# An mLSTM and MLP kernel: items of three pairs in the steady part, a third bank for h, and two banks that scores, sums with v, state update and transposes share

## The chip, the cores and the metric

The kernel runs on one core of one Trainium2 chip. The metric is device time in microseconds (us) of one execution of the whole program; the time before is the median of three runs.

A core has a matrix engine (TensorE, PE in the profile, with its weight loads as PEld), three engines for elementwise work (VectorE or DVE, ScalarE or ACT, GpSimd or POOL) and a queue engine for transfers (SP). They run side by side and wait for each other by semaphores. Products land in PSUM, which has eight banks of 128 partitions x 512 fp32 numbers; everything else lies in SBUF.

## The reference, cut to what matters

```python
# q, k, v: (4, 8, 768, 40); i_gate, f_gate: (4, 8, 768)
for t in range(S):
    m_new = np.maximum(f_gate[:, :, t] + m, i_gate[:, :, t])
    f_stab = np.exp(f_gate[:, :, t] + m - m_new)
    i_stab = np.exp(i_gate[:, :, t] - m_new)
    m = m_new
    C = f_stab[:, :, None, None] * C + i_stab[:, :, None, None] * np.einsum('bhd,bhe->bhde', vt, kt)
    n = f_stab[:, :, None] * n + i_stab[:, :, None] * kt
    h_tilde = np.einsum('bhde,bhe->bhd', C, qt)
    nq = np.einsum('bhd,bhd->bh', n, qt)[:, :, None]
    y[:, :, t] = o * h_tilde / np.maximum(np.abs(nq), 1.0)     # o: sigmoid of o_gate
# x: (3072, 320), tokens by heads and features; w_in: (320, 2048); w_out: (2048, 320)
h = x @ w_in
g = h - np.tanh(h)
out = g @ w_out
```

All of it is fp32. An attention part (the recurrence, done in chunks) makes x, and an MLP with the activation h - tanh(h) makes the output.

## The kernel before, in words

**Tiling.** The 3072 tokens are 24 units of 128 tokens (one batch entry, one chunk of 128 steps). Two units are a group of 256 tokens, so there are 12 groups. The 2048 hidden features are 8 pairs of two blocks of 128. The MLP's work is therefore 12 x 8 pairs (group g, pair p).

**Up.** For one pair, h needs for each of its two blocks i three products into 128 x 256 numbers: two with 128 rows of x (j = 0, 1) and one with the last 64 rows (320 = 128 + 128 + 64). The 64 rows of block 0 lie in the lower half of the array's rows and those of block 1 in the upper half, so two such half products can run at the same time (row tiles). `up` (L748) makes the lists: `full` with the products of 128 rows, and `rest` with the halves.

**Shrink.** `shrink_steps` (L768) makes g from h by a polynomial: per bank of h one square on ACT (which also adds up into a column of `sums`, for a later check of h's size), a second square on ACT, and on DVE a step `cube`, which is the last reader of the bank, and a step `product`. `Clock.later` (L141) puts the DVE steps into the order some time after the squares.

**Down.** For groups 4 to 10 (`SEVEN`), g @ w_out for 2 x 2 blocks is done with seven products in place of eight: `sums_of_weights` (L665) prepares sums of w_out's blocks on DVE (wT, once per pair), `sums_of_g` (L676) sums of g's (s1 to s4; s4 has one buffer), `down_seven` (L687) runs the products of 128 x 160 into three banks, and `put_together` (L722) adds them up. The other groups use `down` (L803) with four products of 128 x 320 per pair.

**Attention of a unit.** `scores` (L552): eight products of 40 rows, also in two row tiles, into two banks, then two masks on DVE. `inter` and `intra` (L577, L586): ph, sums with the state and with v. `gate` (L591): five DVE steps that make y. `update` and `keep_state` (L603, L611): pc, the state, for units that have a later chunk (the last four have none). `turn` and `keep_x` (L620, L628): three transposes px and an ACT copy into xT.

**Order.** All three compute engines run in the order in which the Python code issues (`Pinned`, `T`). The first part (groups 0 to 3, 12 units) is laid out by a planner (`Plan`). From `START` on the steady part is a loop over items (L1125): 64 pairs, in items of two. One item is: its full up products; then the halves together with the scores of a new unit, if one begins (`halves`, L568: products of all parts first, then the shrink steps and masks); then the down products of the item before (LAG = 1). `merge` (L833) strews the remaining attention work of `cell_slot` (L632) between these: 13 slots are spread evenly over the items.

**Banks.** `ph0` and `ph1` take h of an item: bank i holds block i of its pairs. `po0`, `po1` and `b1` take the down sums, `a0` and `a1` the scores, and `b0` in turn ph, pc and px (`small`, L258; `banks[:] = ["b0"]`, L1123).

Of the kernel before, what the change touches and what calls it, by code (L numbers as in the profile page):

```python
# [49 lines left out]
FP = mybir.dt.float32  # L50
# [4 lines left out]
AF = mybir.ActivationFunctionType  # L55
OP = mybir.AluOpType
PSUM = bass.MemoryType.PSUM
NO_SYNC = mybir.DependencyInfo(mybir.DependencyClass.NoSync, mybir.DependencyReason.DATA)

L = 128  # L60
# [18 lines left out]
def kernel(  # L79
# [173 lines left out]
    ps_a = ctx.enter_context(tc.tile_pool(name="ps_a", bufs=1, space=PSUM))  # L253
    ps_b = ctx.enter_context(tc.tile_pool(name="ps_b", bufs=1, space=PSUM))

    banks = ["b0", "b1"]

    def small(shape, name):  # L258
        banks.append(banks.pop(0))
        return ps_b.tile(shape, FP, name=name, tag=banks[-1])  # L260

# [58 lines left out]


    probe = const.tile([128, 1], FP, name="probe")
    V.memset(probe, 0.0)
    A.activation(out=probe, in_=probe, func=AF.Exp)
    ident = const.tile([128, 128], FP, name="ident")
# [328 lines left out]
        return steps + 2 * pause  # L654


    gT, po = {}, {}

# [14 lines left out]

    def sums_of_g(some):  # L676
        a = [[gT[some][i][:, :, tt * L:(tt + 1) * L] for i in range(2)] for tt in range(GT)]
        s1, s2, s3 = (conv.tile([128, 2, L], FP, name=name, tag=tag, bufs=2)[:, 0:len(some)]
                      for name, tag in (("s1", "w_e"), ("s2", "w_m"), ("s3", "w_r")))
        s4 = mlp.tile([128, 2, L], FP, name="s4", tag="s4", bufs=1)[:, 0:len(some)]  # L680
        gS[some] = s1, s2, s3, s4
        V.tensor_tensor(out=s3, in0=a[0][0], in1=a[1][0], op=OP.subtract)
        V.tensor_tensor(out=s1, in0=a[1][0], in1=a[1][1], op=OP.add)
        V.tensor_tensor(out=s2, in0=s1, in1=a[0][0], op=OP.subtract)
        V.tensor_tensor(out=s4, in0=a[0][1], in1=s2, op=OP.subtract)
# [62 lines left out]
    def up(some, shrink):  # L748

        n = len(some)  # L750
        ph = [ps_h.tile([128, 2, TG], FP, name="ph_up", tag=f"ph{i}") for i in range(2)]

        def product(i, x, j):
            g, p = some[x]
            f = 2 * p + i
            at = ((0, 2, 1), (0, 1, 2))[i][j]
            if j < NK:
                lhs, rhs = w_in[:, p, (2 * j + i) * 128:(2 * j + i + 1) * 128], xT[g % NX][:, at, :]
            else:
                rows = slice(i * HALF, (i + 1) * HALF)  # L760
                lhs, rhs = w_in[rows, p, 2 * NK * 128:], xT[g % NX][rows, at, :]
            T.matmul(ph[i][:, x, :], lhs, rhs, start=(x == 0 and j == 0), stop=(j == NK), skip_group_check=True)

        full = [(0.43, lambda i=i, x=x, j=j: product(i, x, j)) for i in range(2) for x in range(n) for j in range(NK)]
        rest = [lambda i=i, x=x: product(i, x, NK) for x in range(n) for i in range(2)]
        return full, (rest, [lambda: shrink(some, ph)])

    def shrink_steps(x, some, ph):  # L768

        n = len(some)  # L770
        z, q = ([mlp.tile([128, 2, TG], FP, name=name, tag=name)[:, 0:n] for i in range(2)] for name in ("z", "q"))
        gt = gT[some] = [mlp.tile([128, 2, TG], FP, name="gt", tag="gt", bufs=4)[:, 0:n] for i in range(2)]

        def square(i):
            A.activation(out=z[i], in_=ph[i][:, 0:n], func=AF.Square, accum_out=sums[:, 2 * x + i:2 * x + i + 1])

        def again(i):
            A.activation(out=q[i], in_=z[i], func=AF.Square, bias=tiny)

        def cube(i):  # L780
            V.scalar_tensor_tensor(out=gt[i], in0=ph[i][:, 0:n], scalar=TINY_POLY[0], in1=z[i], op0=OP.mult, op1=OP.mult)

        def product(i):
            V.scalar_tensor_tensor(out=gt[i], in0=q[i], scalar=TINY_POLY[2], in1=gt[i], op0=OP.add, op1=OP.mult)

        return square, again, cube, product

    def shrink(x):
        def steps(some, ph):
            n = len(some)  # L790
            square, again, cube, product = shrink_steps(x, some, ph)
            for step in (square, again):
                for i in range(2):
                    step(i)
            for i in range(2):
                Clock.later(some, 0.9 + 0.35 * n * i, lambda i=i: cube(i))
                Clock.later(some, 1.0 + 0.75 * n + 0.35 * n * i, lambda i=i: product(i))
            if some[0][0] in SEVEN:
                Clock.later(some, 1.01 + 1.1 * n, lambda: sums_of_g(some))

        return steps

# [54 lines left out]
    items = []  # L857
    while sum(map(len, items)) < len(pairs):
        x = sum(map(len, items))
        items.append(pairs[x:x + (1 if x in ALONE else 2)])  # L860

    assert 2 * len(items) == NS

    def item(x):

# [253 lines left out]
        x0, x1 = (START + (last - START) * j / len(slots) for j in (i, i + 1))  # L1119
        begins[int(x0)].append((slot, x0, x1))  # L1120
    for p in range(NP):
        spread_over([(0.0, lambda p=p: [step() for _, step in sums_of_weights(p)])], START + p / 2, START + 0.5 + p / 2)
    banks[:] = ["b0"]  # L1123
    load_unit(PLANNED)
    for x in range(START, len(items) + LAG):  # L1125
        dense, new = [], []
        for slot, x0, x1 in begins[x]:
            spread_over(cell_slot(*slot), x0, x1)
            if slot[0] is not None:
                new.append(slot[0])  # L1130
# [19 lines left out]

    def rows_of_f():

        xr, n, f = (mlp.tile([L, 2, NR], FP, name=name, tag=tag) for name, tag in (("xr", "z"), ("n", "z"), ("f", "q")))
# [16 lines left out]
        grow = mlp.tile([NR, 2, L], FP, name="grow", tag="gt", bufs=4)  # L1170
        zero = mlp.tile([NR, L], FP, name="zero", tag="gt", bufs=4)
# [65 lines left out]
    lead, root, _, rest = POLY  # L1237

    def shrink_any(ph):
        z = mlp.tile([128, 2, TG], FP, name="z", tag="z")  # L1240
        q = mlp.tile([128, 2, TG], FP, name="q", tag="q")
        t, big = (att.tile([128, 2, TG], FP, name=name, tag="P", bufs=4) for name in ("t", "big"))
        gt = mlp.tile([128, 2, TG], FP, name="gt", tag="gt", bufs=4)
# [11 lines left out]
    with tc.If(nc.values_load(again, min_val=0, max_val=128,  # L1255
                              skip_runtime_bounds_check_because="it counts partitions") > 0):
        T.last = V.last = A.last = None
        banks[:] = ["b0", "b1"]
        un.clear()
        G.tensor_copy(out=diag, in_=ident.unsqueeze(1).to_broadcast([128, H, L]))  # L1260
        V.tensor_copy(out=ei[:, 0], in_=ei[:, 1])
# [88 lines left out]
```

## Time and profile before

| | |
|---|---|
| median of 3 runs | 555.47 us (554.23 to 556.2) |
| profiled execution | 555.52 us, of which 553.7 us lie between its first and its last instruction (the span) |
| TensorE clock granted | 0.997 |
| DMA over the span | 37.97 MB, mean 69 GB/s |
| steady part | 220.8 us to about 547 us |

The busy shares in the page are averages over the whole span. PE records are pipelined: a record's end is modelled and lies after the start of the next, so that lengths in the timeline are read from start to start. An fp32 product leaves two records. `ph_up` is h, `pS` the seven sums, `po` the other down sums, `ps` the scores.

One line of the page on DVE and one on ACT, for the size of the shrink steps:

```profile
L106 DVE SCALAR_TENSOR_TENSOR gt<-ph_up,z 128x512 f32<-128x512 f32 (+1 forms) x100 | 63.3, 662 | 93.1 <-ACT z L106 92.9
...
L106 ACT ACTIVATE q<-z,tiny 128x512 f32<-128x512 f32 (+1 forms) x100 | 64.7, 700 | 0.0
```

After the name of the group stand its count, busy us, mean ns of one, and the engine's idle us before it with what ended most of that.

### The profile page before, as it was taken

How to read it: one execution, taken by the hardware profiler on the slowest of the kernel's cores; microseconds unless marked ns; L12 is line 12 of the kernel's file. 1: busy time of each engine (PE TensorE's matmuls, PEld its weight loads, DVE VectorE, ACT ScalarE, POOL GpSimd, SP SyncE). 2: the span in 40 equal slices, each digit the busy share in tenths (PEclk: the TensorE clock that was granted, in tenths of full speed). 3: DMA queues.
4: the chain of work that ended last, by engine and by line, in shares of the span. 5: the costliest groups of instructions: out<-in, count | busy, mean ns of one | idle time of the engine just before them, and what ended most of it. 6: DMA issues, size and time to landing. Idle time of an engine off the chain costs nothing.

```text
span 553.7 us, 8979 instructions
## 1 busy us (share of the span) xinstructions
PE 539.0 (97%) x3378; PEld 455.6 (82%) x3380; DVE 345.7 (62%) x754; ACT 179.8 (32%) x447; POOL 34.2 (6%) x67
## 2 busy tenths in 40 slices
PE   6999999999999999999999999999999999999995
PEld 4768878787877776798899999999989989988873
DVE  4699888989754335767656647547547547553421
ACT  2444653442432312222232242232233233232331
POOL 6042020320000000000000000000000000000000
PEclk9999999999999999999999999999999999999998
DMA  7789345470310001201202212112110000000000
GB/s 217 203 264 255 113 132 156 155 197 23 95 29 0 1 0 49 83 22 55 85 26 60 62 41 69 47 37 60 49 37 12 1 25 1 1 25 1 24 1 30
DMA packets 39818, 37.97 MB, mean 69 GB/s; under 512 B 3992, under 2 KB 37336, under 8 KB 39768
## 3 DMA queue, kind: packets, MB, share of 16 engines
q1 hardware_dynamic: 32336, 22.24, 14.2%
q0 software_dynamic: 3296, 10.82, 6.4%
q10 hardware_dynamic: 4136, 4.26, 2.2%
q8 instruction: 29, 0.48, 0.4%
q14 instruction: 21, 0.17, 0.1%
HBM read 33.37 MB, written 3.93 MB: 67 GB/s over the span
## 4 chain that ended last, share of the span: by engine, by line
PE 91%; DMA 4%; DVE 3%; issue 1%; SPq 0%; ACT 0%; POOL 0%; DVEq 0%; ACTq 0%
PE ph_up L129 38%; PE pS L129 20%; PE po L129 15%; PE ph L129 9%; PE ps L129 4%; PE pc L129 2%; PE px L133 2%; DMA v<-in_v 1%; DMA kz<-in_kT 1%; DMA q<-in_qT 1%; DVE P L106 1%; DVE w_e L106 1%; DMA w<-in_moe_w_in 0%; DVE gt L106 0%; DVE state L106 0%
## 5 line engine op out<-in xcount | busy, mean ns | idle before, releaser
L129 PE MATMUL ph_up<-xT,w_in 128*128 128x256 f32 (+1 forms) x1152 | 245.4, 391 | 2.1 <-DVE w_in L106 1.3
L129 PEld LDWEIGHTS ph_up<-xT,w_in 128*128 128x128 f32 (+1 forms) x1152 | 169.8, 189 | 35.1 <-issue 12.7
L106 ACT ACTIVATE z<-ph_up 128x512 f32<-128x512 f32 (+1 forms) x100 | 57.1, 576 | 284.2 <-issue 160.6
L106 DVE SCALAR_TENSOR_TENSOR gt<-ph_up,z 128x512 f32<-128x512 f32 (+1 forms) x100 | 63.3, 662 | 93.1 <-ACT z L106 92.9
L129 PE MATMUL po<-w_out,gt 128*128 128x320 f32 x320 | 94.4, 440 | 0.0
L129 PEld LDWEIGHTS po<-w_out,gt 128*128 128x128 f32 x320 | 58.4, 190 | 26.4 <-issue 5.0
L106 DVE TENSOR_TENSOR P<-ps,upto 128x512 f32<-128x512 f32 x48 | 31.5, 683 | 68.2 <-PE ps L129 68.2
L129 PEld LDWEIGHTS ph<-vs,P 128*128 128x128 f32 x384 | 60.1, 202 | 5.7 <-issue 1.5
L106 ACT ACTIVATE q<-z,tiny 128x512 f32<-128x512 f32 (+1 forms) x100 | 64.7, 700 | 0.0
L106 DVE SCALAR_TENSOR_TENSOR gt<-q,gt 128x512 f32<-128x512 f32 (+1 forms) x100 | 63.1, 661 | 1.3 <-ACT q L106 1.3
L129 PE MATMUL ph<-vs,P 128*128 128x41 f32 x384 | 58.9, 273 | 0.0
L129 PE MATMUL pS<-wT,s 128*128 128x160 f32 x336 | 51.3, 300 | 0.0
L129 PEld LDWEIGHTS pS<-wT,s 128*128 128x128 f32 x336 | 47.3, 190 | 0.0
L129 PE MATMUL pS<-w_out,gt 128*128 128x160 f32 x224 | 40.4, 310 | 0.0
L129 PEld LDWEIGHTS pS<-w_out,gt 128*128 128x128 f32 x224 | 32.7, 194 | 1.3 <-issue 1.0
L129 PE MATMUL ps<-qz,kz 40*128 40x128 f32 x384 | 29.6, 291 | 1.7 <-DMA kz<-in_kT 1.5
L129 PEld LDWEIGHTS ps<-qz,kz 40*128 40x128 f32 x384 | 26.9, 199 | 5.0 <-DMA qz<-in_qT 1.8
L458 POOL DMA_DIRECT2D w<-in_moe_w_in x40 | 22.2, 561 | 53.3 <-DVE w_e L106 45.1
L129 PE MATMUL ph<-state,q 120*128 120x123 f32 (+1 forms) x120 | 24.3, 284 | 0.0
L106 ACT COPY xT<-px 128x384 f32<-128x384 f32 x24 | 11.4, 475 | 35.6 <-PE px L133 35.6
L129 PEld LDWEIGHTS ph<-state,q 120*128 120x128 f32 (+1 forms) x120 | 19.9, 191 | 1.5
L106 DVE TENSOR_TENSOR s<-gt 128x256 f32<-128x256 f32 x56 | 21.1, 417 | 0.0
(90 smaller groups left out, 441.0 us busy)
## 6 DMA issues: line engine op xcount, KB each, us to landing
w<-in_moe_w_out POOLq DMA_DIRECT2D x16, 320.0 KB, 5.0
kz<-in_kT SPq DMA_DIRECT2D x48, 80.0 KB
o<-in_o_gate SPq DMA_DIRECT2D x24, 160.0 KB
out<-ob ACTq DMA_DIRECT2D x24, 160.0 KB
k<-in_k SPq DMA_DIRECT2D x20, 180.0 KB
qz<-in_qT SPq DMA_DIRECT2D x44, 80.0 KB
v<-in_v SPq DMA_DIRECT2D x22, 160.0 KB
q<-in_qT SPq DMA_DIRECT2D x40, 60.0 KB
```

Of the source, the lines that this page charges most:

```text
L106: i = method(*args, **kwargs)
L129: return cls.keep(nc.tensor.matmul(*args, **kwargs))
L133: return cls.keep(nc.tensor.transpose(*args, **kwargs))
L458: queue.dma_start(out=to[rows, cols], in_=part)
```

## The change

Steady items take three pairs of a group, then three, then two, so a group has three items and not four. h of the first two pairs stays in `ph0` and `ph1`; the third pair's two blocks share a third bank, `b0`. The rest of the attention work leaves `b0`: ph and px take `a0`, pc takes `a1`, in turn with the scores. For that, the work of a slot is put between 0.75 of the item in which the slot begins and 0.35 of the item in which it ends.

The third pair's half products of the two row tiles go into one bank. The new order is: its first half; the four halves of the other pairs; its second half. A memset on POOL of a one-number tile (`passed`) waits for the first half, and the second half waits for the memset.

Buffers follow: z has three, gt two of three pairs each in place of four of two, s1 to s4 are one pair wider. `sums` keeps its 96 + 4 columns, since a group still has eight banks of h. The due times of the DVE steps grow with the number of banks.

```diff
+SYNC = mybir.DependencyInfo(mybir.DependencyClass.Sync, mybir.DependencyReason.DATA)
...
     def small(shape, name):
+        if name in homes:
+            return ps_a.tile(shape, FP, name=name, tag=homes[name])
         banks.append(banks.pop(0))
...
         n = len(some)
+        wide = n == MOST
         ph = [ps_h.tile([128, 2, TG], FP, name="ph_up", tag=f"ph{i}") for i in range(2)]
+        if wide:
+            ph.append(ps_b.tile([128, 2, TG], FP, name="ph_up", tag="b0"))
...
+            bank, block = (x, i) if x == MOST - 1 else (i, x)
...
-            T.matmul(ph[i][:, x, :], lhs, rhs, start=(x == 0 and j == 0), stop=(j == NK), skip_group_check=True)
+            return T.matmul(ph[bank][:, block, :], lhs, rhs, start=(block == 0 and j == 0), stop=(j == NK), skip_group_check=True)
...
+            def after_the_other():
+                i = product(1, n - 1, NK)
+                tc.add_manual_dep(i.ins, shared[0].ins.name, SYNC, reason="row tiles share a bank")
+
+            def before_the_other():
+                i = product(0, n - 1, NK)
+                shared.append(G.memset(passed, 0.0))
+                tc.add_manual_dep(shared[0].ins, i.ins.name, SYNC, reason="row tiles share a bank")
+
+            rest = [before_the_other, *(lambda i=i, x=x: product(i, x, NK) for x in range(n - 1) for i in (1, 0)), after_the_other]
...
-            for i in range(2):
+            for i in range(m):
                 Clock.later(some, 0.9 + 0.35 * n * i, lambda i=i: cube(i))
-                Clock.later(some, 1.0 + 0.75 * n + 0.35 * n * i, lambda i=i: product(i))
+                Clock.later(some, 1.0 + 0.375 * n * m + 0.35 * n * i, lambda i=i: product(i))
             if some[0][0] in SEVEN:
-                Clock.later(some, 1.01 + 1.1 * n, lambda: sums_of_g(some))
+                Clock.later(some, 1.01 + 0.375 * n * m + 0.35 * n * (m - 1), lambda: sums_of_g(some))
...
-        items.append(pairs[x:x + (1 if x in ALONE else 2)])
+        items.append(pairs[x:x + (1 if x in ALONE else 2 if x < FIRST * NP else min(MOST, NP - x % NP))])
...
-        spread_over([(0.0, lambda p=p: [step() for _, step in sums_of_weights(p)])], START + p / 2, START + 0.5 + p / 2)
-    banks[:] = ["b0"]
+        spread_over([(0.0, lambda p=p: [step() for _, step in sums_of_weights(p)])], START + p / MOST, START + 0.5 + p / MOST)
+    homes.update(ph="a0", pc="a1", px="a0")
...
-            spread_over(cell_slot(*slot), x0, x1)
+            spread_over(cell_slot(*slot), int(x0) + 0.75, int(x1) + 0.35)
```

In this diff `MOST` is 3, n counts pairs (at most two per bank) and m banks.

More of the change, by code (lines that the diff above doesn't have):

```diff
@@ L254 @@
     ps_b = ctx.enter_context(tc.tile_pool(name="ps_b", bufs=1, space=PSUM))
-    banks = ["b0", "b1"]
+    banks, homes = ["b0", "b1"], {}
     def small(shape, name):
+        if name in homes:
+            return ps_a.tile(shape, FP, name=name, tag=homes[name])
         banks.append(banks.pop(0))
@@ L322 @@
     probe = const.tile([128, 1], FP, name="probe")
+    passed = const.tile([1, 1], FP, name="passed")
     V.memset(probe, 0.0)
@@ L654, in cell_slot @@
         return steps + 2 * pause
-    gT, po = {}, {}
+    gT, po, MOST = {}, {}, 3
     HM = DM // 2
@@ L677, in sums_of_g @@
         a = [[gT[some][i][:, :, tt * L:(tt + 1) * L] for i in range(2)] for tt in range(GT)]
-        s1, s2, s3 = (conv.tile([128, 2, L], FP, name=name, tag=tag, bufs=2)[:, 0:len(some)]
+        s1, s2, s3 = (conv.tile([128, MOST, L], FP, name=name, tag=tag, bufs=2)[:, 0:len(some)]
                       for name, tag in (("s1", "w_e"), ("s2", "w_m"), ("s3", "w_r")))
-        s4 = mlp.tile([128, 2, L], FP, name="s4", tag="s4", bufs=1)[:, 0:len(some)]
+        s4 = mlp.tile([128, MOST, L], FP, name="s4", tag="s4", bufs=1)[:, 0:len(some)]
         gS[some] = s1, s2, s3, s4
@@ L761, in product @@
                 lhs, rhs = w_in[rows, p, 2 * NK * 128:], xT[g % NX][rows, at, :]
-            T.matmul(ph[i][:, x, :], lhs, rhs, start=(x == 0 and j == 0), stop=(j == NK), skip_group_check=True)
+            return T.matmul(ph[bank][:, block, :], lhs, rhs, start=(block == 0 and j == 0), stop=(j == NK), skip_group_check=True)
         full = [(0.43, lambda i=i, x=x, j=j: product(i, x, j)) for i in range(2) for x in range(n) for j in range(NK)]
         rest = [lambda i=i, x=x: product(i, x, NK) for x in range(n) for i in range(2)]
+        if wide:
+            shared = []
+            def after_the_other():
[6 more added lines that the diff above has]
+            rest = [before_the_other, *(lambda i=i, x=x: product(i, x, NK) for x in range(n - 1) for i in (1, 0)), after_the_other]
         return full, (rest, [lambda: shrink(some, ph)])
     def shrink_steps(x, some, ph):
-        n = len(some)
-        z, q = ([mlp.tile([128, 2, TG], FP, name=name, tag=name)[:, 0:n] for i in range(2)] for name in ("z", "q"))
-        gt = gT[some] = [mlp.tile([128, 2, TG], FP, name="gt", tag="gt", bufs=4)[:, 0:n] for i in range(2)]
+        n, m = len(some), len(ph)
+        both = mlp.tile([128, MOST, 2, TG], FP, name="gt", tag="gt")
+        gT[some] = [both[:, 0:n, i] for i in range(2)]
+        n = min(n, 2)
+        gt = [both[:, 2] if i == 2 else both[:, 0:n, i] for i in range(m)]
+        z, q = ([mlp.tile([128, 2, TG], FP, name=name, tag=name, bufs=bufs)[:, 0:n] for i in range(m)]
+                for name, bufs in (("z", MOST), ("q", 2)))
+        column = sum(banks_of_item(y) for y in range(x))
         def square(i):
-            A.activation(out=z[i], in_=ph[i][:, 0:n], func=AF.Square, accum_out=sums[:, 2 * x + i:2 * x + i + 1])
+            A.activation(out=z[i], in_=ph[i][:, 0:n], func=AF.Square, accum_out=sums[:, column + i:column + i + 1])
         def again(i):
@@ L789, in steps @@
         def steps(some, ph):
-            n = len(some)
+            n, m = min(len(some), 2), len(ph)
             square, again, cube, product = shrink_steps(x, some, ph)
             for step in (square, again):
-                for i in range(2):
+                for i in range(m):
                     step(i)
-            for i in range(2):
+            for i in range(m):
                 Clock.later(some, 0.9 + 0.35 * n * i, lambda i=i: cube(i))
-                Clock.later(some, 1.0 + 0.75 * n + 0.35 * n * i, lambda i=i: product(i))
+                Clock.later(some, 1.0 + 0.375 * n * m + 0.35 * n * i, lambda i=i: product(i))
             if some[0][0] in SEVEN:
-                Clock.later(some, 1.01 + 1.1 * n, lambda: sums_of_g(some))
+                Clock.later(some, 1.01 + 0.375 * n * m + 0.35 * n * (m - 1), lambda: sums_of_g(some))
         return steps
@@ L859, with banks_of_item @@
         x = sum(map(len, items))
-        items.append(pairs[x:x + (1 if x in ALONE else 2)])
-    assert 2 * len(items) == NS
+        items.append(pairs[x:x + (1 if x in ALONE else 2 if x < FIRST * NP else min(MOST, NP - x % NP))])
+    def banks_of_item(x):
+        return max(2, len(items[x]))
+    assert sum(map(banks_of_item, range(len(items)))) == NS
     def item(x):
@@ L1151, in rows_of_f @@
     def rows_of_f():
-        xr, n, f = (mlp.tile([L, 2, NR], FP, name=name, tag=tag) for name, tag in (("xr", "z"), ("n", "z"), ("f", "q")))
+        xr, n, f = (mlp.tile([L, 2, NR], FP, name=name, tag=tag, bufs=bufs) for name, tag, bufs in (("xr", "z", MOST), ("n", "z", MOST), ("f", "q", 2)))
         V.tensor_single_scalar(xr, lfT.rearrange("p (i c) n -> p i (c n)", i=2), -87.0, op=OP.max)
@@ L1169, in rows_of_f @@
         frow = mlp.tile([NR, 2, L], FP, name="frow", tag="q")
-        grow = mlp.tile([NR, 2, L], FP, name="grow", tag="gt", bufs=4)
-        zero = mlp.tile([NR, L], FP, name="zero", tag="gt", bufs=4)
+        grow = mlp.tile([NR, 2, L], FP, name="grow", tag="gt")
+        zero = mlp.tile([NR, L], FP, name="zero", tag="gt")
         V.memset(zero, 0.0)
@@ L1239, in shrink_any @@
     def shrink_any(ph):
-        z = mlp.tile([128, 2, TG], FP, name="z", tag="z")
+        z = mlp.tile([128, 2, TG], FP, name="z", tag="z", bufs=MOST)
         q = mlp.tile([128, 2, TG], FP, name="q", tag="q")
         t, big = (att.tile([128, 2, TG], FP, name=name, tag="P", bufs=4) for name in ("t", "big"))
-        gt = mlp.tile([128, 2, TG], FP, name="gt", tag="gt", bufs=4)
+        gt = mlp.tile([128, 2, TG], FP, name="gt", tag="gt")
         A.activation(out=z, in_=ph, func=AF.Square)
@@ L1258 @@
         banks[:] = ["b0", "b1"]
+        homes.clear()
         un.clear()
```

## The prediction

> **What bounds the kernel now.** I read the page's engine table, then its chain of waits, to see which engine sets the end.
>
> ```profile
> PE 539.0 (97%) x3378; PEld 455.6 (82%) x3380; DVE 345.7 (62%) x754; ACT 179.8 (32%) x447; POOL 34.2 (6%) x67
> ...
> PE 91%; DMA 4%; DVE 3%; issue 1%; SPq 0%; ACT 0%; POOL 0%; DVEq 0%; ACTq 0%
> ```
>
> TensorE is busy for 97% and holds 91% of the chain. A busy PE may still hide waits, so I asked for windows: is any stretch of the steady part (from 220.8 us) not full?
>
> ```profile
> 200.00:250.00 50.00, 49.22 (x281) 39.47 (x278) 31.05 (x76) 14.62 (x38) 0.00 (x0) 1.00 0.14 44
> ...
> 300.00:350.00 50.00, 50.00 (x353) 45.98 (x353) 28.50 (x63) 13.00 (x35) 0.00 (x0) 1.00 0.17 51
> ```
>
> The columns are length, then busy time and count of PE, PEld, DVE, ACT and POOL, clock, DMA. PE loses 0.78 us at one place in the steady part; POOL does nothing there. The changed part can win only what PE itself wastes. The chain in order of time shows that, where no attention work lies between:
>
> ```profile
> 490.00 4.52 PE ph_up L129 x24
> 494.52 4.00 PE pS L129 x28
> 498.52 4.52 PE ph_up L129 x24
> 503.04 4.00 PE pS L129 x28
> ```
>
> An fp32 product leaves two records. The timeline at 313.62 to 314.49 gives 0.87 us for two whole up products, 0.433 each; twelve records, six products, of the s downs from 311.45 to 313.08 give 0.272 each. A two-pair item has 8 whole up products and 4 half ones, which run two at a time: 8 x 0.433 + 2 x 0.433 = 4.33 us, against 4.52. Its 14 down products make 14 x 0.272 = 3.81, against 4.00. So PE pays about 0.19 us on going into the 64-row halves and 0.19 on coming out, 0.39 per visit (rounded once). In the timeline 128x41 products cost about 0.22 us more wherever they are put in, so their place is worth nothing.
>
> **What the Trainium skill says.** "TensorEngine Tiling (Array Packing)", Tiling Modes, Key Properties: "Changing tiling mode (not just tile) drains the TensorE". The 0.39 us agrees. The same page, Restrictions and Gotchas, says that different row tiles can't write one PSUM bank at the same time, and that software must keep them apart; this case's third bank takes both halves, and no run here shows what happens without the order. "GPSIMD Engine Reference", section 3.1, says that an instruction passes two software dispatch hops there and one on VectorE. The trace agrees: POOL starts 0.29 us after the DVE result that it waits for, PE 0.05 us (first line ends 45.91, PE starts 45.96; third ends 69.15, POOL starts 69.44):
>
> ```profile
> 45.42 0.49 DVE L106 TENSOR_TENSOR state<-pc,eT 120x328 f32<-120x328 f32 x1
> ...
> 45.96 0.58 PE L129 MATMUL pc<-vs,k 128*120 128x123 f32 x3 [0.49 <-DVE state L106]
> ...
> 68.33 0.82 DVE L106 SCALAR_TENSOR_TENSOR w_e<-w,w_e 128x640 int32<-128x640 int32 x1
> ...
> 69.44 0.56 POOL L458 DMA_DIRECT2D w<-in_moe_w_out  x1 [15.60 <-DVE w_e L106]
> ...
> 0.31 0.10 POOL L1342 MEMSET const-float32-0.0<- 128x1 f32 x1 [0.31 <-issue]
> ```
>
> "SBUF — State Buffer", Who interferes with whom, lets a GpSimd write wait for DVE only where DVE runs a 2-port mode (copies, tensor_scalar). DVE's groups in the steady part are TENSOR_TENSOR, SCALAR_TENSOR_TENSOR and small reciprocals, so I charge nothing for the port; no run shows it.
>
> **The change, part by part.**
>
> *Removed: visits to the halves.* Eight groups had 4 items each, now 3 (3, 3 and 2 pairs): 32 visits become 24. All products, 64 ACT squares, 64 second squares, 128 DVE shrink steps and their sizes stay; in the built order every attention score still lies in such a visit. 8 x 0.39 = 3.1 us. Twelve of the old visits came out into a transpose (px at 318.89, 0.16 instead of 0.11 us, then nothing), cheaper by about 0.04 than the usual exit; no new one does: 12 x 0.04 = 0.5. **Gain 2.6 us.** The sums for the seven-product rule become 84 instructions instead of 112 on DVE; DVE isn't the bound, so nothing.
>
> *Added: a wait in 16 items.* The third pair's two halves share a bank. The built PE order is: first half of pair 3, then four halves of pairs 1 and 2, then the second half of pair 3, waiting for a POOL memset that waits for the first. Behind it on PE stand the scores or the next down products, so all wait. Cover: the halves go as three couples, and between the end of couple 1 and the start of couple 3 lies one couple, 0.43 us. The turn: a half's last pass starts 0.22 before its couple ends, and its record takes 0.38, so its end is 0.16 after couple 1; POOL 0.29; memset 0.10; back to PE 0.05; then the first weights load that can no longer hide, 0.10 (half of the 0.19 above). 0.16 + 0.29 + 0.10 + 0.05 + 0.10 = 0.70, less 0.43 is 0.27. Lower bound: if POOL reacts as DVE does to PE (a mask starts 0.03 after the scores' end) the sum is 0.44, so 0.01. Upper: the built program gives POOL two waits, PE and its own last memset; at 0.29 each it is 0.56. I take 0.28, because the 0.29 is what POOL shows each time it waits for DVE. **Cost 16 x 0.28 = 4.5 us** (0.2 to 9). POOL's queue holds nothing else there.
>
> *Moved: the start of the steady part.* Before, PE waits there for the first cube, behind which DVE's order shows why:
>
> ```profile
> 229.47 4.76 PE L129 MATMUL ph_up<-xT,w_in 128*128 128x256 f32 x24 [0.78 <-DVE gt L106]
> ...
> 226.38 1.29 DVE L106 TENSOR_TENSOR P<-ps,upto 128x512 f32<-128x512 f32 x2 [2.95 <-PE ps L129]
> 227.58 0.32 DVE L106 TENSOR_TENSOR wT<-w_out 128x160 f32<-128x160 f32 x1
> ...
> 228.65 0.68 DVE L106 SCALAR_TENSOR_TENSOR gt<-ph_up,z 128x512 f32<-128x512 f32 x1
> 229.25 0.48 DVE L106 TENSOR_TENSOR ob<-po,part 128x320 f32<-128x320 f32 x1
> 229.65 0.68 DVE L106 SCALAR_TENSOR_TENSOR gt<-ph_up,z 128x512 f32<-128x512 f32 x1
> ```
>
> In the new DVE order a scaling vs (0.40 from start to next start) stands between the masks and cube 0: the first stall becomes 0.78 + 0.40 = 1.18. Then cube 0, ob, cube 1, ob, four wT and cube 2 follow: 0.60 + 0.40 + 0.60 + 0.40 + 1.07 = 3.07 us from cube 0's end to cube 2's, while PE, which needs the third bank after four whole products, gets there in 4 x 0.433 = 1.73. Second stall 1.34. **Cost 0.40 + 1.34 = 1.7 us**, once. Later PE has at least one item's downs and four up products between the scores and the third bank, 3.8 + 1.7 = 5.5 us, and DVE two masks and three cubes, 1.2 + 1.8 = 3.0 (up to 1.07 more with a wT): covered.
>
> *Moved: attention into the scores' banks.* The second product chain ph and transposes px take a0, state update pc takes a1, and each slot runs from 0.75 of one item to 0.35 of a later one. In eight of the twelve units three pc products and pauses separate gate and transposes, and the gate's 1.64 us (311.33 to 312.96) is covered. The last four have no update. In two of these (the short slots) the built orders put the gate behind s4 and vs on DVE, s4 behind the last down product, and the transposes only one ph and four whole up products after it. PE: 0.27 + 0.22 + 1.73 = 2.2 us. DVE: product's end 0.44 after its start, s4 0.47 (estimate between 0.42 at 256 and 0.68 at 512 columns, less overlap), vs 0.40, gate 1.64, then 0.15 to PE: 3.1. At most 0.9, at least 0.5 if s4 starts earlier; I take 0.75 each. **Cost 1.5 us.** Moved DMAs: each unit's loads are still issued a whole slot (at least one item, 8.5 us) ahead; a unit's issues fill about 6 us of SP. Nothing.
>
> The tail keeps a two-pair item and its downs. Sum: -2.6 + 4.5 + 1.7 + 1.5 = **+5.1 us**. The profiled execution took 555.5 us (span 553.7), the median shown is 555.47, so both give 560.6.
>
> **Rivals.**
> 1. *POOL answers at once.* Speaks for it: the memset is 0.10 us and POOL idle; against: the 0.29. The wait then costs 0.2 in all, the stalls stay: -2.6 + 0.2 + 3.2 = +0.8, 556.3 us, not told from no change (about 0.3%, 1.7 us, is what a measurement of this kernel can tell).
> 2. *Faster: fewer mode changes with every wait covered.* As rival 1, and DVE's first cubes come in time because the DVE work ahead of them overlaps more than the rows say. -2.6 + 0.2 = -2.4, 553.1 us. It decides if POOL's start is under 0.1 us after PE's result and both early stalls vanish; the 0.78 already there speaks against.
> 3. *POOL takes two turns*, or the second half runs alone for its 0.43: 16 x 0.56 = 9.0 in place of 4.5, 565.1 us.
> 4. *DVE becomes the bound in the short slots*: the 0.75 falls on five more units, +3.8, 564.4 us. For: s4 holds DVE behind PE; against: their updates leave over 1 us.
>
> **How the numbers follow.** Forecast 0.60, rival 1 0.13 (three parts of four inside 0.3%, the rest slower), rival 2 0.07, rival 3 0.13, rival 4 0.07. Slower 0.60 + 0.03 + 0.13 + 0.07 = 0.83, same 0.10, faster 0.07. The forecast's own bounds without rival 3 are about 557.5 to 563; with rivals 1, 4 and half of 3 the range is 556.0 to 564.8.
>
> **What would show it.** Right: PE gaps of about 0.28 us inside 16 half visits, ended by POOL; gaps near 1.2 and 1.3 us at the second steady item; two gaps before px late; a two-pair item without attention still at 4.52 and 4.00. Wrong: half visits without a gap, or an item whose up part waits for DVE again and again.

## The result and the profile after

| | before | after |
|---|---|---|
| median | 556.89 us (18 runs, 554.23 to 558.29) | 558.78 us (18 runs, 557.73 to 561.89) |
| ratio after to before | | 1.0044, interval 1.003 to 1.0058 |
| profiled execution | 555.52 us (span 553.7) | 560.2 us (span 558.0) |
| steady part, first up product to last down product | 325.73 us (from 220.77) | 328.73 us (from 222.06) |

The change makes the kernel slower: by the ratio of the runs 0.44% or 2.5 us (its interval is 1.7 to 3.2 us), while the two medians of the table lie 1.9 us apart. The forecast said slower by 5.1 us, 560.6 us in a range of 556.0 to 564.8: the sign was right and the time lies inside the range, but the size was about twice too large. The profiled pair differs by 4.7 us, more than the medians. 1.3 us of that lie ahead of 222.06 us, where PE, DVE, ACT and POOL have the same order of instructions in both kernels: the runs below, which leave that order as it is too, begin their steady part between 219.9 and 223.6 us, and one of them, built on the kernel before, at 222.7. From the start of the last down product to the span's end it is 7.2 us in both. What is to be explained is the steady part, **+3.0 us**, and all lengths below are of that part, each from one profiled execution. Visits of the same kind and place in it agree within 0.002 us.

The engine table and the chain, after:

```profile
PE 542.4 (97%) x3378; PEld 459.1 (82%) x3380; DVE 345.3 (62%) x726; ACT 181.2 (32%) x447; POOL 35.5 (6%) x83
...
PE 91%; DVE 5%; DMA 1%; issue 1%; SPq 0%; ACT 0%; POOL 0%
```

TensorE still sets the end. POOL holds nothing of the chain, although 16 waits for it are new. Windows over exactly the steady part, before and then after (length, then busy time and count of PE, PEld, DVE, ACT and POOL, clock, DMA):

```profile
220.77:546.50 325.73, 324.95 (x2165) 288.61 (x2163) 186.99 (x417) 92.09 (x236) 0.00 (x0) 1.00 0.12 35
```

```profile
222.06:550.78 328.72, 324.98 (x2164) 289.95 (x2163) 186.06 (x389) 93.40 (x236) 1.41 (x16) 1.00 0.12 35
```

PE's busy time is the same within 0.03 us; its idle time grew from 0.78 to 3.74. It would be wrong to read from this that saved visits and added POOL waits are both worth nothing. The Trainium skill, "Perfetto Trace Analysis", Tensor Engine Instruction, says that a TensorE record's end is estimated from the instruction's size, so that its time "is a model, not a measurement". This trace agrees: a wait of a tenth of a microsecond inside a visit lies under the end of the record before it and counts as busy, and so does the first part of every longer gap. Saved visits, hidden waits and these parts cancel to 0.03 here, and each has to be read from start to start. The idle part can be read at once, from the waits of PE (us in total, times, longest):

```profile
PE ph_up L130 <- DVE gt L107: 2.2, 2, 1.1
...
PE px L134 <- DVE ys L107: 2.0, 3, 0.8
```

Before, these rows were 0.8 in one wait and 0.5 in one. So four gaps are in the steady part, 1.15 and 1.09 us for the cube steps (at 233.3 and 236.4 us), and 0.75 twice for ys (at 423.5 and 465.7); the wait of 0.5 for ys lies ahead of it. From start to start, less the product's own time, they cost 1.31, 1.25, 0.92 and 0.92 us, together 4.40, against 0.94 for the one of before: **+3.45 us**. The product behind such a wait is late as well: its second record starts 0.29 us after its first at a cube wait, in place of 0.22, and the record behind a late transpose comes 0.14 us after it in place of 0.11. That is +0.13 us more.

The visits are seen in the chain in order of time, where no attention stands between:

```profile
501.12 4.52 PE ph_up L130 x24
505.64 5.90 PE pS L130 x42
511.54 6.77 PE ph_up L130 x36
518.31 4.00 PE pS L130 x28
```

The two-pair item keeps its 4.52 and 4.00. The three-pair item's down products take 5.90 = 21 x 0.272 + 0.19, as they should. Its up part has 12 whole products and 3 couples of halves, 15 x 0.433 = 6.50; 6.77 leaves 0.27 where a visit into the halves costs 0.19. The rest, 0.08 us, is the wait for POOL. The same from the records: a visit without scores takes, from its first half to the first full-array product, 1.064 us with four halves and 1.587 with six. The third couple adds 0.523, of which 0.43 is its own time: 0.09. A visit with scores takes 2.479 us, again 0.09 more than 1.957 + 0.433; only the first of the 16, with 2.420, pays 0.03. Together the wait costs **1.4 us**, not 4.5.

The last term is counted visit by visit, from start to start and less the products' own times. A visit between whole products costs 0.09 us where it is entered, 0.20 inside and 0.10 where it is left, 0.39 to 0.40 in all. After the change all 24 visits are entered and left at about this price, 9.5 us, without POOL's part. Before, the 32 visits together cost 11.4, 0.36 on average. Twelve of them are left into a transpose, for 0.06 in place of 0.10, and nine are entered behind a 128x41 product, for 0.02 in place of 0.09:

```profile
306.62 0.31 PE L129 MATMUL ph<-vs,P 128*128 128x41 f32 x2
306.87 1.13 PE L129 MATMUL ph_up<-xT,w_in 64*128 64x256 f32 x8
```

Before rounding the two starts are 0.242 us apart, where such a product elsewhere (0.22) and an ordinary entry (0.09) make 0.31. An exit into a 128x41 product isn't cheap: all twelve cost 0.10. So the eight visits fewer saved **2.0 us** (1.95). -1.95 + 1.38 + 3.45 + 0.13 = +3.0, as measured.

### The profile page after: what moved, and what is told of

It reads as the page before. It is cut to its first block, busy times and chain, and to the rows that moved or that the text cites. A ratio compares the mean times of both kernels' runs of the same rounds, so it can differ in the third digit from the quotient of the medians.

```text
span 558.0 us, 8884 instructions
## 1 busy us (share of the span) xinstructions
PE 542.4 (97%) x3378; PEld 459.1 (82%) x3380; DVE 345.3 (62%) x726; ACT 181.2 (32%) x447; POOL 35.5 (6%) x83
## 4 chain that ended last, share of the span: by engine, by line
PE 91%; DVE 5%; DMA 1%; issue 1%; SPq 0%; ACT 0%; POOL 0%
PE ph_up L130 38%; PE pS L130 21%; PE po L130 15%; PE ph L130 9%; PE ps L130 4%; PE pc L130 2%; PE px L134 1%; DMA kz<-in_kT 1%; DVE gt L107 1%; DVE P L107 0%; DVE w_e L107 0%; DVE den L107 0%; DVE o L107 0%; DMA w<-in_moe_w_in 0%; PE awake L130 0%
## 5 line engine op out<-in xcount | busy, mean ns | idle before, releaser
L130 PE MATMUL ph_up<-xT,w_in 128*128 128x256 f32 (+1 forms) x1152 | 239.8, 391 | 2.7 <-DVE gt L107 2.2
L130 PEld LDWEIGHTS ph_up<-xT,w_in 128*128 128x128 f32 (+1 forms) x1152 | 175.1, 190 | 38.9 <-issue 17.3
L130 PE MATMUL pS<-wT,s 128*128 128x160 f32 x336 | 63.0, 311 | 0.0
L130 PEld LDWEIGHTS pS<-wT,s 128*128 128x128 f32 x336 | 48.9, 191 | 0.0
L130 PE MATMUL pS<-w_out,gt 128*128 128x160 f32 x224 | 36.3, 307 | 0.0
L130 PEld LDWEIGHTS pS<-w_out,gt 128*128 128x128 f32 x224 | 31.1, 190 | 3.3 <-issue 2.0
L130 PE MATMUL ps<-qz,kz 40*128 40x128 f32 x384 | 31.5, 297 | 0.6 <-DMA kz<-in_kT 0.4
L130 PEld LDWEIGHTS ps<-qz,kz 40*128 40x128 f32 x384 | 28.8, 204 | 3.6 <-issue 1.2
L107 DVE SCALAR_TENSOR_TENSOR den<-ph,inv 128x8 f32<-128x8 f32 x24 | 3.9, 164 | 35.8 <-PE ph L130 35.8
L107 DVE TENSOR_TENSOR s<-gt,s 128x384 f32<-128x384 f32 (+1 forms) x21 | 10.8, 514 | 22.9 <-PE pS L130 22.2
```

What stands on the lines that cost most here:

```text
L107: i = method(*args, **kwargs)
L130: return cls.keep(nc.tensor.matmul(*args, **kwargs))
```

## The experiments

Every ratio is to the kernel before, timed on the same chip in the same rounds. The first group removes one cost each; the second measures the terms of the sum by themselves.

### The two early waits for VectorE

The sums of w_out's blocks (wT) stand ahead of the cubes in DVE's order, at the only place where the third bank is needed so early. The edit issues the sums of the first four pairs earlier; for pairs 2 and 3 it takes them out of the cubes' way:

```diff
-        spread_over([...sums_of_weights(p)...], START + p / MOST, START + 0.5 + p / MOST)
+        spread_over([...sums_of_weights(p)...], START + (p / 20 if p < 4 else p / MOST), START + 0.5 + p / MOST)
```

> The weight sums of pairs 2 and 3 run on VectorE before the masks of the first steady item, where it idles; all else as in the changed kernel. Theory (the two early gaps of the changed kernel, 1.31 us at the first and 1.25 us at the third bank of the second steady item, exist because eight wT steps, 2.1 us, stand between the masks and the third cube): both gaps shrink to below 0.4 us, so 2.0 us less than the changed kernel, about 1.0010 of the kernel before. Rival (VectorE's work is only moved, and TensorE meets the same lateness at the next wait, the first sums of g): the gaps go, another of 1 to 2 us appears within the next 15 us, and the time is that of the changed kernel, 1.0044.

Measured: 556.76 us (before 556.44), ratio 1.001, 0.9997 to 1.0023; steady part 326.60 us, 2.13 less than the changed kernel. DVE's timeline of the changed kernel, around the gaps (start, length, operation):

```profile
230.43 0.68 DVE L107 TENSOR_TENSOR P<-ps,upto 128x512 f32<-128x512 f32 x1
231.03 0.31 DVE L107 TENSOR_TENSOR wT<-w_out 128x160 f32<-128x160 f32 x1
...
232.09 0.48 DVE L107 TENSOR_TENSOR vs<-v,ei 128x320 f32<-128x320 f32 x1
232.49 0.68 DVE L107 SCALAR_TENSOR_TENSOR gt<-ph_up,z 128x512 f32<-128x512 f32 x1
...
233.49 0.68 DVE L107 SCALAR_TENSOR_TENSOR gt<-ph_up,z 128x512 f32<-128x512 f32 x1
234.09 0.48 DVE L107 TENSOR_TENSOR ob<-po,part 128x320 f32<-128x320 f32 x1
234.48 0.31 DVE L107 TENSOR_TENSOR wT<-w_out 128x160 f32<-128x160 f32 x1
...
235.54 0.68 DVE L107 SCALAR_TENSOR_TENSOR gt<-ph_up,z 128x512 f32<-128x512 f32 x1
```

Beside it PE's, whose brackets give the idle time and what ended it:

```profile
233.32 1.97 PE L130 MATMUL ph_up<-xT,w_in 128*128 128x256 f32 x8 [1.15 <-DVE gt L107]
236.37 1.97 PE L130 MATMUL ph_up<-xT,w_in 128*128 128x256 f32 x8 [1.09 <-DVE gt L107]
```

PE goes on when the first cube is done, and stops again after its four whole products until the third cube frees the third bank. DVE has no hole here: four wT and one vs stand ahead of the first cube, four wT ahead of the third. With the edit DVE does this:

```profile
228.84 1.29 DVE L107 TENSOR_TENSOR P<-ps,upto 128x512 f32<-128x512 f32 x2 [2.36 <-PE ps L130]
230.04 0.48 DVE L107 TENSOR_TENSOR vs<-v,ei 128x320 f32<-128x320 f32 x1
230.44 0.69 DVE L107 SCALAR_TENSOR_TENSOR gt<-ph_up,z 128x512 f32<-128x512 f32 x1
...
232.43 0.68 DVE L107 SCALAR_TENSOR_TENSOR gt<-ph_up,z 128x512 f32<-128x512 f32 x1
```

The third cube now follows the first after 1.99 us instead of 3.05, and the row of waits for gt is gone from PE's list. From start to start 0.25 and 0.19 us are left of the two gaps. The wT found room in DVE's 2.36 us of idle time before the masks. Nothing took their place: the wait was one of order, not of load.

### The waits for ys

In the short slots the gate stands on DVE behind s4, which waits for PE's down products. The edit puts seven pauses where other slots have their state update, so that the transposes come later in PE's order:

```diff
         if o + B < NU:
             steps += [(0.2, lambda j=j: update(o, j)) for j in range(len(TRIOS))] + 4 * pause
+        else:
+            steps += (len(TRIOS) + 4) * pause
```

> Units without a state update get seven more pause steps before their transposes; all else as in the changed kernel. Theory (the two gaps of 0.92 us before px, units 20 and 22, exist because the gate on VectorE starts late behind s4 and only four up products cover it): both gaps go, 1.8 us less than the changed kernel, about 1.0011 of the kernel before. Rival (the bank a0 is now given back later, so the scores of the next unit wait for the copy out of px): the gaps move to the scores, 0.5 to 1.5 us each, and nothing is won.

Measured: 557.98 us, ratio 1.0031, 1.0018 to 1.0044; steady part 327.50, 1.23 less than the changed kernel where 1.8 was expected. Each gap shrank from 0.92 to 0.31, not to nothing: half a hit. The order of the changed kernel on DVE shows both causes:

```profile
420.82 0.56 DVE L107 TENSOR_TENSOR s<-gt,s 128x384 f32<-128x384 f32 x1 [1.43 <-PE pS L130]
421.30 0.48 DVE L107 TENSOR_TENSOR vs<-v,ei 128x320 f32<-128x320 f32 x1
421.70 0.16 DVE L107 SCALAR_TENSOR_TENSOR den<-ph,inv 128x8 f32<-128x8 f32 x1
...
422.85 0.49 DVE L107 TENSOR_TENSOR ys<-ph,o 128x320 f32<-128x320 f32 x1
```

DVE waits 1.43 us for PE at s4 (which has one buffer), and then PE waits for DVE, 0.75 us, at the first transpose at 423.49. From s4's start to ys's start are 2.03 us. With the pauses the gate comes right behind s4 and vs behind the gate, so the chain is 0.40 shorter, and the transpose stands one whole product (0.43) later in PE's order. A 128x41 product of 0.22 us that stood between the last down product and the up products is no longer there, so the gap shrinks by 0.40 + 0.43 - 0.22 = 0.61:

```profile
420.07 0.56 DVE L107 TENSOR_TENSOR s<-gt,s 128x384 f32<-128x384 f32 x1 [1.64 <-PE pS L130]
420.55 0.16 DVE L107 SCALAR_TENSOR_TENSOR den<-ph,inv 128x8 f32<-128x8 f32 x1
...
421.70 0.49 DVE L107 TENSOR_TENSOR ys<-ph,o 128x320 f32<-128x320 f32 x1
```

A few more pauses should hide the rest; the last experiment tries that.

### The wait for POOL, hidden behind scores

In seven of the 16 wide visits eight scores follow the halves. The edit puts four of them, all of one row group, ahead of the late half, and the other four beside it:

```diff
+    def visit(rest, *parts):
+        if len(rest[0]) == 6 and parts:
+            (s, masks), = parts
+            rest, parts = (rest[0][:-1] + s[1::2] + rest[0][-1:] + s[0::2], rest[1]), (([], masks),)
+        halves(rest, *parts)
...
-            dense.append((0.6 + 0.9 * len(new[:1]), lambda: halves(rest, *(scores(n) for n in new[:1]))))
+            dense.append((0.6 + 0.9 * len(new[:1]), lambda: visit(rest, *(scores(n) for n in new[:1]))))
```

> In the seven three-pair visits that hold scores, four of the eight score products are put between the first and the second half product of the third bank, and four beside the second; all else as in the changed kernel. Theory (the wait through GpSimd is exposed by 0.10 us in each of 16 visits, and more cover hides it): these seven visits end 0.10 us earlier, 0.7 us in all, about 1.0031 of the kernel before; the nine others keep the 0.10. Rival (the 0.10 is the price of pairing a late half with the scores, not of the wait): the visits keep their length, 1.0044.

A miss: 559.9 us (seven runs), ratio 1.0063, 1.0039 to 1.0086, and a steady part of 330.60. The seven visits grew from 2.479 (the first from 2.420) to 2.734 us. The memset is now done 0.85 us before the late half's weight load (0.91 in the first visit), so the wait itself is gone; the edit broke the pairing. Four scores of one row group are eight passes of 0.111 us, 0.89 us in order, but the half that could run beside them takes only 0.43. So half of that stretch has one row group empty. The mistake lay in the size of the filling, so a second form takes two scores (four passes, 0.44 us) ahead of the late half and two beside it:

```diff
+            rest, parts = (rest[0][:-1] + s[1:4:2] + rest[0][-1:] + s[0:4:2] + s[4:], rest[1]), (([], masks),)
```

> Against the changed kernel only the order inside the seven visits with scores is other: two score products of row group 1 stand between the two halves (passes in order, so 4 x 0.111 = 0.44 us, the time of one half), the other two of that group beside the second half. Theory: the wait for POOL is hidden behind those two products and the pairs of halves still run side by side, so these visits take 2.39 us from the first half's record to the first full-array record, not 2.479; 7 x 0.09 = 0.6 us less than the changed kernel, ratio to before about 1.0033. Rival: a half beside two scores costs extra whatever the order, then the visits take 2.48 or more and the ratio stays at 1.0044 or above.

In the trace this is what the theory said to the last digit: seven visits of 2.389 to 2.391 us in place of 2.479 (2.420 in the first), and the nine without scores unchanged at 1.587. The steady part is 328.19, 0.53 less than the changed kernel: six times 0.09, while PE loses the 0.03 of the first visit again in the cube wait behind it. The time of the whole can't show so little: 558.04 us (six runs) against 555.33, ratio 1.0054, 1.0034 to 1.0074; the expected 1.0033 lies just outside it and the changed kernel's 1.0044 inside. That the wait is hidden there rests on the visits' lengths, not on this ratio.

### POOL's turn, doubled

A second memset stands behind the first, and the late half waits for the second:

```diff
                 shared.append(G.memset(passed, 0.0))
+                shared.append(G.memset(passed, 0.0))
...
-                tc.add_manual_dep(i.ins, shared[0].ins.name, SYNC, reason="row tiles share a bank")
+                tc.add_manual_dep(i.ins, shared[-1].ins.name, SYNC, reason="row tiles share a bank")
```

> The changed kernel with two memsets on GpSimd, one after the other, between the first and the second half product of the third bank. Theory (the turn through GpSimd is a chain of its steps, each 0.085 to start and 0.088 to run as the trace of the changed kernel shows, and it lies bare on TensorE): 0.17 us more in each of 16 visits, 2.8 us more than the changed kernel, about 1.0094 of the kernel before. Rival (GpSimd takes the second memset while the first is still on its way, 0.03 us apart as its first memsets in the profile of before are): 16 x 0.03 to 0.05, 0.5 to 0.8 us more, 1.0053 to 1.0058.

Measured: 560.98 us (before 556.41), ratio 1.0101, 1.0076 to 1.0126; steady part 330.90, 2.2 more than the changed kernel. POOL's timeline in one visit, and the chain at a visit with no attention:

```profile
285.18 0.09 POOL L784 MEMSET passed<- 1x1 f32 x1 [11.66 <-PE ph_up L130]
285.33 0.09 POOL L785 MEMSET passed<- 1x1 f32 x1
```

```profile
514.99 6.91 PE ph_up L130 x35
521.90 4.00 PE pS L130 x28
```

The second memset starts 0.146 us after the first, and the item's up part grows from 6.77 to 6.91. All of it lies bare on PE: the cover is used up, and what POOL takes beyond it costs its full price. 15 x 0.145 = 2.2 us, where 16 x 0.17 = 2.8 were expected; the first visit's 0.145 shortens the cube wait behind it, from 1.15 to 1.00 us idle.

### The price of a visit, doubled

The edit is made to the kernel before: each of its 32 steady items now goes into the halves twice, for two halves each time. Nothing is left out or added:

```diff
+        if n == 2 and some[0][0] >= FIRST:
+            full[6:6] = [(0.2, step) for step in rest[:2]]
+            rest = rest[2:]
```

> The kernel before, but in each of the 32 steady items the two half products of the first pair run as a visit of their own, before the last two whole up products; the same products in all. Theory (each visit to the row tiles costs 0.39 us in going in and out, whatever it holds): 32 x 0.39 = 12.5 us more than the kernel before, 1.022. Rival (most of the 0.39 is paid only because of what follows, scores or down products, and whole up products on both sides hide it): 0 to 6 us, 1.000 to 1.011.

Measured: 569.4 us, ratio 1.0249, 1.0217 to 1.028; steady part 337.60, 11.87 more. The wait for the first cube, 0.94 us from start to start before, is gone from PE's list in this run, so the 32 added visits cost 11.87 + 0.94 = 12.8 us, 0.40 each. The chain shows it item by item, where before had 4.52:

```profile
506.37 4.00 PE pS L129 x28
510.37 4.92 PE ph_up L129 x24
```

4.92 is 4.52 + 0.40. The price of a visit is real and as large as the prediction had it.

### The banks alone

Items of two pairs again, with the changed kernel's use of the banks and its slots. No third bank of h, no wait for POOL:

```diff
-        wide = n == MOST
+        wide = n > 2
...
-        items.append(pairs[...2 if x < FIRST * NP else min(MOST, NP - x % NP))])
+        items.append(pairs[...2 if x < FIRST * NP else 2)])
...
-        spread_over([...sums_of_weights(p)...], START + p / MOST, START + 0.5 + p / MOST)
+        spread_over([...sums_of_weights(p)...], START + p / 2, START + 0.5 + p / 2)
```

> Items of two pairs as before, no third bank and no wait through GpSimd, but the attention work in the banks of the scores and the slots cut as in the change. Theory (sharing the two banks costs nothing by itself, since no slot is short here: 13 slots over 26 items; the costs of the change come from the third bank and from the short slots): within 0.6 us of the kernel before, 0.999 to 1.001. Rival (scores, masks and ph queue for the two banks and TensorE waits at each change of user): at least one gap of 0.2 us per unit, 12 units, 2.4 us or more, 1.004 or above.

A miss for both theories: 557.69 us, ratio 1.0026, 1.0013 to 1.0038; steady part 327.08, 1.35 more than before. There are no gaps at a change of the banks' user. One part is the first wait for the cube, 1.2 us in PE's list in place of 0.8, since vs stands ahead of the cube here as in the changed kernel (+0.40). The other is the visits: 12.35 us in 32 of them, 0.39 each, in place of 11.4 and 0.36 (+0.94). With the later slots none of the visits is left into a transpose any more (+0.57), and four in place of nine are entered behind a 128x41 product (+0.37). In the changed kernel none of the 24 is entered so, which costs it 9 x (0.093 - 0.018) = 0.7 us. This is what the saving of 2.0 in place of 2.6 comes from; the twelve cheap exits are gone there too, but those the prediction had counted. That these neighbours are what makes a visit cheap is read from the traces' start-to-start lengths; no run moved them alone.

### All together

First the three edits (four scores, wT early, seven pauses) in one kernel:

> The three edits together: early weight sums, later transposes for units without an update, scores between the halves. Theory (the costs of the changed kernel are separate and additive on TensorE): 2.0 + 1.8 + 0.7 = 4.5 us less than the changed kernel, some 2.1 us less than the kernel before, 0.996 of it; no gap of TensorE over 0.4 us in the steady part. Rival (VectorE or a bank is the next bound): at least half of it stays, 0.999 to 1.003.

A miss again: 557.73 us, ratio 1.0022, 1.0009 to 1.0035; steady part 327.26. No idle gap over 0.2 us is left, but the seven long visits of the four-score form cost their 1.8 us here too. With the two-score form, and thirteen pauses where seven were (`TRIOS` has three entries):

```diff
+        else:
+            steps += (len(TRIOS) + 10) * pause
```

> The scores' order of the run before this one, with the sums of weights started earlier and the state update at a later turn. Theory: the three costs found are separate, so -2.1 (two early waits for VectorE) -1.8 (waits for ys at the third bank's products) -0.6 (seven visits) = -4.5 us against the changed kernel: about 324.2 us in the steady part against 325.7 before, ratio to before 0.996 to 0.998. Rival: removing one wait brings another (VectorE is late anyway), then the steady part stays at 325.7 or above and the ratio at 1.000 or above.

Measured: 554.01 us (22 runs) against 555.33 (27 runs), ratio 0.9975, 0.9962 to 0.9988; steady part 324.17 us against 325.73, where 324.2 was expected. It beats both kernels, by a quarter of a per cent over the kernel before. PE's longest waits in this run, all of them ahead of the steady part:

```profile
PE awake L130 <- DVE diag L107: 2.1, 1, 2.1
PE ps L130 <- DMA kz<-in_kT: 0.6, 1, 0.6
PE gate L130 <- ACT ei L107: 0.5, 1, 0.5
PE px L134 <- DVE ys L107: 0.5, 1, 0.5
PE ph_up L130 <- DVE w_in L107: 0.4, 2, 0.2
```

The row for gt is gone and ys is back at its one wait of the first part. The three costs were separate, and none brought another. What is left of POOL's turn are the nine visits without scores, 9 x 0.09 = 0.8 us, and of the two cube waits 0.28 and 0.19 us from start to start.

## Why the prediction was half right, point by point

**What bounds the kernel.** Right. TensorE sets the end, and time is won or lost only in its visits and gaps.

**Fewer visits, 2.6 us gained.** The price of 0.39 a visit was right (0.40 when doubled). Measured 2.0. The step allowed 0.5 for the exits into a transpose, and they make 0.57. It allowed nothing for the nine entries behind a 128x41 product, 0.7 us. That the place of these products "is worth nothing" was the wrong sentence.

**The wait for POOL, 4.5 us.** The mechanism was right and the size of one term was wrong, and this is the largest error of the sum: 3.1 us. The chain was put at 0.16 + 0.29 + 0.10 + 0.05 + 0.10 = 0.70, less 0.43 of cover. In the visit at 282.52 us the records say: the second couple starts at 283.054; the first half ends at 283.214 (0.16 later, as predicted); POOL's memset starts at 283.337 (**0.12, not 0.29**); it takes 0.09; the weight load follows 0.05 after it; and the late half's second pass is 0.10 late, as predicted. 0.16 + 0.12 + 0.09 + 0.05 + 0.10 = 0.52, less 0.43 is 0.09.

```profile
283.34 0.09 POOL L784 MEMSET passed<- 1x1 f32 x1 [11.66 <-PE ph_up L130]
```

Up to the weight load the turn takes 0.42 us and just fits under the cover; what shows is the load.

The 0.29 was read from transfers that POOL starts after a DVE result; a memset after a PE result isn't that. Which of the two differences counts, the transfer or the engine waited for, these runs don't separate. That "the trace agrees" compared POOL's transfer with a product of PE, and doesn't carry over to the memset. The Trainium skill, "Perfetto Trace Analysis", DMA Instruction — SWDGE (GPSIMD), says that such a transfer's instruction doesn't read a tensor, so that the profiler shows little of it and no start of its own. The trace of the kernel before does print one (69.44); how far it can be read as the start, no run shows. The page's warning on GpSimd spans (GPSIMD Engine Instruction: take the spacing from start to start) holds for the split of the 0.26 us between PE's record and PE's weight load too. Firm are the delay of 0.09 on PE and the spacing of 0.146 between two memsets.

The text itself put the lower bound at 0.03 for this term, and the truth lay between, nearer to it. The upper bound, a second 0.29 for POOL's wait for its own last memset, was wrong by far: the first of the 16 memsets has no such wait and starts 0.064 us after the half's end, the others 0.122 to 0.123, and its visit is 0.06 us shorter (2.420 against 2.479). So half of the 0.12 is this second wait. Whether a tile for each memset would save it was not tried.

**The start of the steady part, 1.7 us.** Right: 1.31 + 1.25 - 0.94 = 1.62, for the named reasons (vs ahead of the first cube, four wT ahead of the third), and moving the wT alone took 2.1 of the 2.56 us away.

**Transposes in the short slots, 1.5 us.** Right in place and cause: two gaps, in two of the four units without an update. They cost 0.92 each from start to start, 1.84. The prediction's own working, in starts, gave 3.1 - 2.2 = 0.9, which was right; the 0.75 was chosen below it, for a case in which s4 starts earlier. That PE's idle time reads 0.75 too is chance: it is short by what the modelled end of the record before it takes.

**Nothing from shared banks otherwise, nothing from DMA or DVE's load.** Right: no other gap appeared. Rival 4, DVE as the bound, didn't come up; rival 1, POOL at once, was nearer on its term (0.2 us, where 1.4 was measured and 4.5 forecast); rival 2's condition on POOL was nearly met (0.12 us against its 0.1), but not that on the early stalls. The order edits of the last run then reached its side of the result.

**The sum.** The errors went both ways: POOL's term was 3.1 us too high, visits and the ys gaps together 1.0 too low. With POOL's term right, the forecast would have been +2.0 us, less than was measured. So the sum came nearer to the result than its largest term did, and that was luck; the sign didn't depend on it.

| term | predicted, us | measured, us |
|---|---|---|
| visits fewer | -2.6 | -1.95 |
| POOL's turn | +4.5 | +1.38 |
| two early gaps | +1.7 | +1.62 |
| two gaps for ys | +1.5 | +1.84 |
| late products behind the gaps | | +0.13 |
| sum | +5.1 | +3.0 |

## What to carry to other kernels

The latency of a hand-over between two engines should be read from the same pair and the same kind of instruction, and where no such row exists, the number at hand is a bound and not the forecast: here 0.29 was for a transfer, and with the memset it was 0.12, between it and the lower reading of 0.03. When a larger tile saves something on the bounding engine, look for what the in-order queues of the others put ahead of its new first use; such a wait cost nothing to remove here, since that engine had room elsewhere. And a filling for a wait must have the length of what runs beside it: two scores hid the wait in full, four made it worse than no filling.

## What the runs showed that was not expected

- A hand-over from PE through a POOL memset back to PE takes 0.12 us to its start, 0.09 for the memset and 0.05 back; 0.06 of the 0.12 are the wait on POOL's own earlier memset. A further memset adds 0.145.
- Going into 64-row tiles and back costs PE 0.39 to 0.40 us where full-width products stand on both sides. The entry is 0.09 of it, but 0.02 behind a 128x41 product; the exit is 0.10, but 0.06 into a transpose.
- Start-to-start time counts, not the waits' idle time: gaps shown as 1.15, 1.09 and twice 0.75 us cost 1.31, 1.25 and 0.92.
